# Attention in pairs of 64-row products, the low-rank mixer's sums after attention, the norm's preparation a step earlier

## The chip, the cores and the metric

The kernel runs on one core of a Trainium2 chip. The metric is device time in microseconds of one execution, the median of several runs. The engines are PE (TensorE, the matrix products, with its weight loads shown apart as PEld), DVE (VectorE), ACT (ScalarE), POOL (GpSimd) and SP (SyncE, which here only issues DMAs).

## The reference

Three blocks follow each other on a batch of 2, with 3136 tokens and 256 features, all in float32:

```
# 1 attention, z has 64 features
attn = max((z @ z.T) / S, 0) ** 2
x    = u * (attn @ v)
# 2 low-rank token mixer (rank 32), then a channel block of width 1024
u  = x + (x.T @ U @ V).T
x  = u + max(u @ w1a, 0) @ w2a
# 3 real part of a 2-d Fourier transform, norm, channel block of width 1024
u  = x + real(fft2(x));  un = (u - mean) / sqrt(var + 1e-6)
out = u + max(un @ w1b, 0) @ w2b
```

U, V and the channel weights are float64 and are converted on the chip. Every float32 factor is split into a high part h (rounded to the fast matmul format) and a low part l = x - h, and a product is the sum of h·h, h·l and l·h.

## The kernel before

The work is written out by hand in program order: each engine takes its instructions in the order in which Python emits them, and generators (`active`) are advanced once a step to weave side work in between.

**Attention** (`attention`) goes over 2 batches, 7 query chunks of 448 queries (`qc`), and 13 steps `p` of 256 keys (the last has 64 keys). `scores(b, qc, p)` fills a PSUM tile of two banks: T1 holds zh in rows 0 to 63 and zl in rows 64 to 127, T2 the same with the halves exchanged, so two products over all 128 rows (L541, L542) give all four parts for 128 keys. ACT then does Relu (L547) and Square (L550), DVE the high part (L551) and the low part (L96). `values(b, qc, p)` adds three products (L571, L573, L574) for each of two feature halves and two key tiles into two accumulators. In step 12 the 64 keys stand twice in the rows, so two score products and four value products do. Scores run two steps ahead of values (LAG = 2); at step 12, the turn, values come first, then `gate` (multiply by u, write to DRAM), then the scores. After the gate of a second chunk, `mixing` begins: PE transposes the gated tiles (L607), ACT and DVE split them, and PE sums them with U (L628), woven into attention's steps; the last ones (`tail`) run beside the first channel chunk. `finish_G` replicates the sums (L216). The conversions of the float64 weights are woven in as well; those of w1b (`conv_w`, not second) have a product with ones (L506).

**Channel blocks.** Fourteen chunks of 448 tokens for block 2 and fourteen for block 3, each in 8 steps: `hidden(k)` six products (L329 to L331), `project(k)` two steps later six more (L354 to L356). `Chunk.load` brings a chunk of x and of V from DRAM on SP; `prep1` or `prep2` runs during the chunk before, from its step 2, one piece a step: `prep1` adds the mixer's part, `prep2` makes the mean and the variance (row sum L302, three small DMAs on POOL's queue at L306, L319 and L321) and leaves 1/std in `rs`, which `finish` needs. `fourier(0)` and `fourier(1)` run beside the chunks; `features` waits for two `row` DMAs on POOL's queue (L953) that go out at the last of a group's pairs.

PSUM has eight banks: in attention two for misc and the mixer's sum (`pmg`), four for scores, two for the accumulators.

Of the kernel before, what the change touches and what calls it, by code (L numbers as in the profile page):

```python
# [15 lines left out]
ALU = mybir.AluOpType  # L16
# [66 lines left out]
def program(ctx, tc, zT, v, uT, U, V, w1a, w2a, w1b, w2b, b49, f64, fd, rep, mask, out):  # L83
# [18 lines left out]
    pmg = ctx.enter_context(tc.tile_pool(name="pmg", bufs=1, space=PSUM))  # L102
# [17 lines left out]
    V_d = dram.tile([RANK, S], F32, tag="Vd", name="Vd")  # L120
# [13 lines left out]
    Utail = const.tile([128, 4, 64], F32R, name="Utail")  # L134
# [67 lines left out]
    misc_pools = [(pmg, "m")]  # L202
# [8 lines left out]
    def finish_G(b, g, P):  # L211
        nc.vector.memset(P[64:128], 0.0)
        nc.vector.tensor_copy(P[0:64], g[0:64, 0:D])
        yield
        ps = pmg.tile([128, 512], F32, tag="m", name="ps_m")
# [7 lines left out]
    class Chunk:  # L223
# [4 lines left out]
        def load(self, a):  # L228
            self.a = a
            load(out=a, in_=aT_d[self.b][:, :, self.sl].rearrange("a p n -> p a n"))  # L230
            self.vr = com.tile([128, CH], F32, tag="Vr", name="Vr", bufs=1)
            for k in range(4):
                load(out=self.vr[k * 32 : k * 32 + 32, :], in_=V_d[:, self.sl])
# [4 lines left out]
        def prep1(self):  # L238
            b, a, vr = self.b, self.a, self.vr
            vs = com.tile([128, CH], F32R, tag="Vs", name="Vs", bufs=1)  # L240
            hcopy(vs, vr)
            for k in (32, 96):
                sub(vs[k : k + 32, :], vr[k : k + 32, :], f(vs[k : k + 32, :]))
# [30 lines left out]
        def prep2(self):  # L274
# [24 lines left out]
            yield  # L299

            ps = misc()
            mm(ps[0:1, 0:CH], ones[:, 0:1], st, start=True, stop=True)  # L302
            row = mp.tile([1, CH], F32, tag="vrow", name="vrow", bufs=1)
# [3 lines left out]
            yield  # L307
# [11 lines left out]
            late_dma(out=row_d.rearrange("(p j) -> p j", j=4), in_=y)  # L319
            self.rs = mp.tile([128, CH], F32, tag="rs", name="rs")  # L320
# [64 lines left out]
    def attention(stack):  # L385
# [5 lines left out]
        T1, T1d, T2, Vt, uq = {}, {}, {}, {}, {}  # L391
        zraw, vraw = {}, {}
        Uhl = att.tile([128, 25, 2, RANK], F32R, tag="U", name="Uhl", bufs=1)

        def load_z(b, c):
            raw = att.tile([128, CH], F32, tag="zraw", name="zraw")
            for h, dma in enumerate((load, nc.scalar.dma_start if (b, c) == (0, 0) else load)):
                dma(out=raw[h * 64 : h * 64 + 64, :], in_=zT[b, :, c * CH : c * CH + CH])
            zraw[b, c] = raw

        def split_z(b, c):
            raw = zraw.pop((b, c))
            if c == 0:
                T1[b] = big.tile([128, S], F32R, tag="T1", name=f"T1_{b}")
            dst = T1[b][:, c * CH : c * CH + CH]
            hcopy(dst, raw)
            if (b, c) == (0, 0):
                t = T2[0, 0] = att.tile([128, CH], F32R, tag="T2", name="T2")
                hcopy(t[64:128], raw[64:128])
                sub(dst[64:128], raw[64:128], f(dst[64:128]))  # L410
                sub(t[0:64], raw[0:64], f(dst[0:64]))
            else:
                sub(dst[64:128], raw[64:128], f(dst[64:128]))
            if c == NC - 1:
                T1d[b] = att.tile([128, 2, 64], F32R, tag="T1d", name=f"T1d_{b}")
                for h in range(2):
                    nc.vector.tensor_copy(T1d[b][:, h, :], f(T1[b][:, S - 64 : S]))

        def load_q(b, qc):
            t = att.tile([128, CH], F32R, tag="T2", name="T2")  # L420
            for h in range(2):
                nc.gpsimd.dma_start(
                    out=t[h * 64 : h * 64 + 64, :],
                    in_=T1[b][64 - h * 64 : 128 - h * 64, qc * CH : qc * CH + CH],
                )
            T2[b, qc] = t
# [24 lines left out]
        def conv_U(k):  # L451
# [14 lines left out]
            if k >= 3:  # L466
                o, i = ((3, 0), (0, 3))[k - 3]
                nc.vector.tensor_copy(
                    Utail[:, i : i + n - o], f(t[:, o:].rearrange("p a h n -> p a (h n)"))
                )  # L470

        def conv_V(k):
# [7 lines left out]
            load(out=quarter(V_d, 1), in_=y)  # L480

        def conv_w(src, k, second, dst):
# [13 lines left out]
            if not second:  # L496
                both = f(raw[:, 0:128])
                tt(out=both, in0=y[:, 0:128], in1=y[:, 128:256], op=ALU.add)
                yield
                yield  # L500
                while mixes:
                    yield
                mixes.append(k)

                ps = misc()
                mm(ps[:, 0:128], f(ones), both, start=True, stop=True)  # L506
                for a in range(2):
                    sub(y[:, a * 128 : a * 128 + 128], y[:, a * 128 : a * 128 + 128], ps[:, 0:128])
            load(out=dst[k], in_=y)
            if not second:  # L510
                yield
                mixes.remove(k)
# [17 lines left out]
        def scores(b, qc, p):  # L530
            n = 2 if p < 12 else 1
            ps = psS.tile([128, 2, 512], F32, tag="S", name="psS")
            q1 = T1[b][:, qc * CH : qc * CH + CH]
            q2 = T2[b, qc]
            for j in range(n):
                k = (
                    T1[b][:, (2 * p + j) * 128 : (2 * p + j) * 128 + 128]
                    if p < 12
                    else T1d[b].rearrange("p a n -> p (a n)")
                )  # L540
# [4 lines left out]
            parts = ((0, 1), (1, 1)) if (b, qc, p) == (0, 0, 0) else ((0, n),)  # L545
            for j, m in parts:
                act(out=c2(A)[:, j : j + m], in_=ps[:, j : j + m, 0:CH], func=AF.Relu, scale=1.0 / S)  # L547
            for j, m in parts:
                w = slice(j * CH, (j + m) * CH)
                act(out=A[:, w], in_=A[:, w], func=AF.Square)  # L550
                nc.vector.tensor_copy(h[:, w], A[:, w])  # L551
                if p < 12:
                    sub(l[:, w], A[:, w], f(h[:, w]))
                else:
                    sub(h[64:128, w], A[64:128, w], f(h[64:128, w]))
            prob[b, qc, p] = (h, l)

        acc = {}

        def values(b, qc, p):  # L560
            if p == 0:
                acc[b, qc] = [psO.tile([128, 512], F32, tag=f"O{a}", name=f"psO{a}") for a in range(2)]
            o = acc[b, qc]
            h, l = prob.pop((b, qc, p))
            vt = Vt[b, p]
            for a in range(2):
                dst = o[a][:, 0:CH]
                for j in range(2 if p < 12 else 1):
# [489 lines left out]
```

## Time and profile before

| | |
|---|---|
| median of 3 runs | 1218.4 us (1217.89 to 1220.7) |
| the profiled execution | 1218.11 us |
| its span in the trace | 1216.3 us |
| PE busy, PEld busy | 99%, 91% of the span |
| DVE, ACT, POOL busy | 68%, 54%, 4% |
| DMA | 68.56 MB, mean 56 GB/s |

The span is the time between the first and the last instruction of the trace; the device time has 1.8 us around it. PE's busy time is a union of overlapping products, so the spacing of their starts tells more than their lengths. Attention takes the first half, the channel blocks the second.

### The profile page before, as it was taken

To read this page: it belongs to the slowest core of one execution; us is meant where nothing else is said; L and a number is where in the kernel's file an instruction comes from. 1 tells how busy PE (TensorE), PEld (TensorE's weight loads), DVE (VectorE), ACT (ScalarE), POOL (GpSimd) and SP (SyncE) were. 2 spreads that over 40 slices of the span, in tenths; PEclk is the share of its full clock that TensorE was granted. 3 is DMA by queue.
4 is the path that set the end of the run, shared out by engine and by line. 5 is a ranking of instruction groups with operands and counts; after the bars stand their busy time and mean duration, and the time that the engine had idled before them with its cause. 6 is when DMAs were issued, how large, how long until landed. Compare 5 with 4: busy or idle time off the path is not lost.

```text
span 1216.3 us, 16363 instructions
## 1 busy us (share of the span) xinstructions
PE 1202.9 (99%) x6038; PEld 1102.4 (91%) x6038; DVE 829.8 (68%) x1565; ACT 652.5 (54%) x1052; POOL 46.8 (4%) x94
## 2 busy tenths in 40 slices
PE   9999999999999999999999999999999999999998
PEld 7999999999999999999899998999989889999997
DVE  7867777888666667666555456476576688666664
ACT  7767667777666566665433334333255444444442
POOL 0000000000000000000000000000000101000100
PEclk9999999999999999999999999999999999999999
DMA  5302220333122012211111102212012111111111
GB/s 153 104 22 69 68 64 26 117 93 105 44 64 64 9 57 77 60 40 54 38 51 53 46 23 85 81 45 62 5 57 73 48 39 31 39 31 38 31 39 46
DMA packets 58688, 68.56 MB, mean 56 GB/s; under 512 B 11630, under 2 KB 53712, under 8 KB 58608
## 3 DMA queue, kind: packets, MB, share of 16 engines
q1 hardware_dynamic: 54144, 61.13, 16.4%
q0 software_dynamic: 4384, 6.27, 2.6%
q8 instruction: 47, 0.77, 0.3%
q14 instruction: 33, 0.27, 0.1%
q10 hardware_dynamic: 80, 0.11, 0.0%
HBM read 44.86 MB, written 19.56 MB: 53 GB/s over the span
## 4 chain that ended last, share of the span: by engine, by line
PE 90%; DVE 4%; issue 3%; DMA 1%; ACT 1%; POOL 0%; SPq 0%; DVEq 0%; POOLq 0%; ACTq 0%
PE psO L574 12%; PE psO L571 12%; PE psO L573 11%; PE psH L330 6%; PE psH L329 6%; PE psH L331 6%; PE psC L355 6%; PE psC L354 6%; PE psC L356 6%; PE psS L542 6%; PE psS L541 6%; PE ps_g L628 1%; PE ps_m L607 1%; DVE Hl L335 1%; DVE l L96 0%
## 5 line engine op out<-in xcount | busy, mean ns | idle before, releaser
L571 PE MATMUL psO<-h,Vt 128*128 128x448 f32 x700 | 256.6, 367 | 0.1
L574 PE MATMUL psO<-h,Vt 128*128 128x448 f32 x700 | 256.5, 366 | 0.0
L573 PE MATMUL psO<-l,Vt 128*128 128x448 f32 x672 | 246.3, 367 | 0.3 <-DVE l L96 0.2
L547 ACT ACTIVATE P<-psS 128x896 f32<-128x896 f32 (+1 forms) x183 | 161.6, 884 | 147.7 <-PE psS L542 147.2
L335 DVE SCALAR_TENSOR_TENSOR Hl<-psH,Hh 128x448 fp32r<-128x448 f32 x224 | 139.6, 623 | 142.7 <-ACT Hh L334 141.6
L334 ACT ACTIVATE Hh<-psH 128x448 fp32r<-128x448 f32 x224 | 121.8, 544 | 200.2 <-PE psH L331 197.1
L96 DVE TENSOR_TENSOR l<-P,h 128x896 fp32r<-128x896 f32 (+1 forms) x197 | 201.2, 1021 | 23.5 <-ACT h L93 17.7
L551 DVE CAST h<-P 128x896 fp32r<-128x896 f32 (+1 forms) x183 | 111.0, 606 | 145.7 <-ACT P L550 144.6
L550 ACT ACTIVATE P<-P 128x896 f32<-128x896 f32 (+1 forms) x183 | 168.4, 921 | 5.7
L329 PE MATMUL psH<-h,w 128*128 128x448 f32 x448 | 167.9, 375 | 0.0
L330 PE MATMUL psH<-l,w 128*128 128x448 f32 x448 | 164.5, 367 | 0.2 <-DVE l L96 0.2
L331 PE MATMUL psH<-h,w 128*128 128x448 f32 x448 | 164.5, 367 | 0.0
L355 PE MATMUL psC<-Hl,w 128*128 128x448 f32 x448 | 163.7, 365 | 0.0
L354 PE MATMUL psC<-Hh,w 128*128 128x448 f32 x448 | 163.7, 365 | 0.0
L356 PE MATMUL psC<-Hh,w 128*128 128x448 f32 x448 | 163.2, 364 | 0.0
L571 PEld LDWEIGHTS psO<-h,Vt 128*128 128x128 f32 x700 | 131.6, 188 | 11.4 <-DVE aT L586 0.6
L574 PEld LDWEIGHTS psO<-h,Vt 128*128 128x128 f32 x700 | 131.6, 188 | 11.2 <-DVE Vt L96 0.3
L573 PEld LDWEIGHTS psO<-l,Vt 128*128 128x128 f32 x672 | 126.4, 188 | 11.3 <-DVE l L96 0.9
L541 PE MATMUL psS<-T 128*128 128x448 f32 x336 | 125.2, 373 | 0.8 <-DVE T L96 0.8
L542 PE MATMUL psS<-T,T 128*128 128x448 f32 x336 | 124.2, 370 | 0.0
L329 PEld LDWEIGHTS psH<-h,w 128*128 128x128 f32 x448 | 84.7, 189 | 7.9 <-ACT h L93 0.3
L331 PEld LDWEIGHTS psH<-h,w 128*128 128x128 f32 x448 | 84.4, 188 | 7.3
(276 smaller groups left out, 1421.8 us busy)
## 6 DMA issues: line engine op xcount, KB each, us to landing
uT<-in_uT SPq DMA_DIRECT2D x14, 448.0 KB, 4.2
vraw<-in_v SPq DMA_DIRECT2D x24, 256.0 KB, 2.7
out<-P SPq DMA_DIRECT2D x27, 224.0 KB, 2.0
aTd<-aT SPq DMA_DIRECT2D x13, 448.0 KB, 3.0
P<-aTd SPq DMA_DIRECT2D x13, 448.0 KB, 3.6
scr<-wst SPq DMA_DIRECT2D x16, 256.0 KB, 2.0
Vr<-Vd SPq DMA_DIRECT2D x56, 56.0 KB, 3.0
rs<-rsd POOLq DMA_DIRECT2D x14, 224.0 KB, 3.6
```

Source lines behind the costliest of these rows:

```text
L96: tt(out=o, in0=a, in1=b, op=ALU.subtract)
L329: mm(ps[:, 0:CH], wh, self.h[:, a], start=a == 0, stop=False)
L330: mm(ps[:, 0:CH], wh, self.l[:, a], start=False, stop=False)
L331: mm(ps[:, 0:CH], wl, self.h[:, a], start=False, stop=a == 1)
L354: mm(dst, wh, h, start=k == 0, stop=False)
L355: mm(dst, wh, l, start=False, stop=False)
L356: mm(dst, wl, h, start=False, stop=k == 7)
L541: mm(ps[:, j, 0:CH], k, q1, start=True, stop=False)
L542: mm(ps[:, j, 0:CH], k, q2, start=False, stop=True)
L571: mm(dst, vh, hj, start=p == 0 and j == 0, stop=False)
L573: mm(dst, vh, lj, start=False, stop=False)
L574: mm(dst, vl, hj, start=False, stop=p == 12)
```

## The change

Attention's products take 64 rows each. Keys 0 to 127 of a step lie in rows 0 to 63 of KT and keys 128 to 255 in rows 64 to 127, and the queries stand in both halves, so the scores are three products (h·h, l·h, h·l) for each half, issued alternately. The value products are cut into their upper and lower 64 rows, each with an accumulator of its own; `gate` adds the two. At step 12 the scores have 224 columns, and feature half 1 of step 11 is put behind feature half 0 of step 12. The queries are read from DRAM again for every chunk and split (at steps 4 and 8) instead of copied on POOL's queue.

```diff
 def scores(b, qc, p):
-    for j in range(n):
-        mm(ps[:, j, 0:CH], k, q1, start=True, stop=False)
-        mm(ps[:, j, 0:CH], k, q2, start=False, stop=True)
+    w = CH if p < 12 else CH // 2
+    for kk, kq in ((0, 0), (1, 0), (0, 1)):
+        for j, r in enumerate(halves):
+            ...
+            mm(ps[:, j, 0:w], k, q[r, kq, o : o + w], start=(kk, kq) == (0, 0), stop=kq == 1)
+def products(b, qc, p, a):
+    if p < 12:
+        todo = [(j, (a, k, x), (a, k, x)) for j in range(2) for k, x in ((0, h), (0, l), (1, h))]
+    elif a == 0:
+        todo = [(0, (0, 0, h), (0, 0, l)), (0, (0, 1, h), (1, 1, h))]
+    else:
+        todo = [(0, (1, 0, h), (1, 0, l))]
+    for n, (j, *both) in enumerate(todo):
+        for i, (fa, k, x) in enumerate(both):
+            r = halves[i]
+            mm(o[fa][i][:, 0:CH], vt[r, j, k, fa * 128 : fa * 128 + 128], x[r, j * CH : j * CH + CH], ...)
 def gate(b, qc):
+    t = att.tile([128, 2, CH], F32, tag="aT", name="aT")
     for a in range(2):
-        tt(out=t[:, a], in0=o[a][:, 0:CH], in1=u[:, a], op=ALU.mult)
+        hcopy(t[:, a], o[a][0][:, 0:CH])
+        tt(out=t[:, a], in0=o[a][1][:, 0:CH], in1=t[:, a], op=ALU.add)
+    tt(out=t, in0=t, in1=u, op=ALU.mult)
     load(out=aT_d[b][:, :, qc * CH : qc * CH + CH].rearrange("a p n -> p a n"), in_=t)
```

The mixer no longer runs beside attention, nor does w1b's product with ones (it moves into `weights(0)`, beside channel chunks 2 to 5). All of x is read into SBUF in four DMAs behind attention, after four short early ones for the first 1536 tokens of batch 0; the mixer of both batches then runs before the first channel chunk, and the chunks take x from there. The four early DMAs go out at step 11 of the last query chunk; `first` is what is left of batch 0's mixer and then the first chunk's `prep1`.

```diff
+                    if p == NP - 2:
+                        for k in range(4):
+                            t = ptile().rearrange("p (a n) -> p a n", a=2)[:, :, 0:384]
+                            load(out=t, in_=aT_d[0][:, :, k * 384 : k * 384 + 384].rearrange("a p n -> p a n"))
+                            early.append(t)
+    for b in range(NB):
+        for s in (slice(1536, S), slice(0, 1536)):
+            load(out=xT[b][:, :, s], in_=aT_d[b][:, :, s].rearrange("a p n -> p a n"))
+    def mixer(b):
+        for k in range(25):
+            ps = misc()
+            for a in range(2):
+                ...
+                nc.tensor.transpose(ps[:, a * 128 : a * 128 + 128], t, ident)
+            hcopy(h, ps[:, 0:D])
+            sub(l, ps[:, 0:D], f(h))
+            ready.append((k, h, l))
+            if k > 1:
+                sums(*ready.pop(0))
+        ...
+        yield from finish_G(b, g, ...)
+        mix0, mix1 = mixer(0), mixer(1)
+        for _ in range(13):
+            next(mix0)
+        last_G = mix0
+        opening = [mix1, first()]
+        while opening:
+            for g in list(opening):
+                if next(g, "end") == "end":
+                    opening.remove(g)
```

V is split once when it is converted and is loaded as h and l on POOL's queue. In `prep2` one step is put between the stacked squares and the row sum L302, one is taken away behind the DMA of the variances, and one is put between the write of 1/std to DRAM and the DMA that reads it back into `rs`; it begins at step 1 of the chunk before and not at step 2. In `fourier` the first transposes come a step later, and the `row` DMAs go out at a group's first pair (in the first group at its second):

```diff
-                if g == pairs[-1]:
+                if g == max(1, pairs[0]):
...
-            if k == 2 and c + 1 < len(chunks):
+            if c + 1 < len(chunks) and k == 3 - chunks[c + 1].layer:
...
                 active.insert(0, chunks[c + 1].prep())
```

The products that warm PE up at the start become twenty 64-row ones.

## Rows read from the trace of the kernel before

**Rows 1.** The page: span, busy engines, bytes per slice, chain of waits
```profile
span 1216.3 us, 16363 instructions
PE 1202.9 (99%) x6038; PEld 1102.4 (91%) x6038; DVE 829.8 (68%) x1565; ACT 652.5 (54%) x1052; POOL 46.8 (4%) x94
...
GB/s 153 104 22 69 68 64 26 117 93 105 44 64 64 9 57 77 60 40 54 38 51 53 46 23 85 81 45 62 5 57 73 48 39 31 39 31 38 31 39 46
...
PE 90%; DVE 4%; issue 3%; DMA 1%; ACT 1%; POOL 0%; SPq 0%; DVEq 0%; POOLq 0%; ACTq 0%
```

**Rows 2.** Groups by line, PE: count, busy us, mean ns, idle before
```profile
L506 PE MATMUL ps_m<-stg,ones 128*128 128x128 f32 x16 | 3.1, 273 | 0.0
```

**Rows 3.** Timeline, PE, twelve value products: start us, length us
```profile
591.17 0.36 PE L571 MATMUL psO<-h,Vt 128*128 128x448 f32 x1
...
593.61 0.36 PE L250 MATMUL ps_m<-Vs,Gs 128*128 128x448 f32 x1
```

**Rows 4.** Timeline, PE, two products that follow each other
```profile
767.18 0.37 PE L354 MATMUL psC<-Hh,w 128*128 128x448 f32 x1
767.39 0.37 PE L355 MATMUL psC<-Hl,w 128*128 128x448 f32 x1
```

**Rows 5.** Timeline, PEld (weight loads), the same stretch and 0.8 us on
```profile
767.18 0.19 PEld L355 LDWEIGHTS psC<-Hl,w 128*128 128x128 f32 x1
...
767.80 0.19 PEld L822 LDWEIGHTS ps_x<-nl,b49h 98*128 98x128 f32 x1
767.91 0.19 PEld L823 LDWEIGHTS ps_x<-nh,b49l 98*128 98x128 f32 x1
768.02 0.19 PEld L329 LDWEIGHTS psH<-h,w 128*128 128x128 f32 x1
```

**Rows 6.** Timeline, PE, four transposes and four sums of the mixer
```profile
104.34 0.60 PE L607 MATMUL ps_m<-ident,aT 128*128 128x128 f32 x4
...
105.25 0.37 PE L541 MATMUL psS<-T 128*128 128x448 f32 x1
```

**Rows 7.** Groups by line, ACT and DVE, splits of 256 columns
```profile
L93 ACT CAST anh<-ps_m 128x256 fp32r<-128x256 f32 x8 | 3.0, 373 | 5.5 <-PE ps_m L607 5.5
...
L96 DVE TENSOR_TENSOR Tl<-ps_x,Th 128x256 fp32r<-128x256 f32 x10 | 4.2, 417 | 0.0
```

**Rows 8.** Windows: busy us of each engine, then PEclk, DMA share, GB/s
```profile
555.00:560.00 5.00, 5.00 (x26) 4.54 (x25) 3.58 (x6) 4.25 (x5) 0.00 (x0) 1.00 0.64 203
950.00:960.00 10.00, 7.44 (x31) 6.76 (x30) 4.47 (x10) 3.90 (x8) 1.60 (x3) 0.83 0.13 27
```

**Rows 9.** DMA issues by line: count, KB each, median us from issue to landing
```profile
P<-aTd SPq DMA_DIRECT2D x13, 448.0 KB, 3.6
```

**Rows 10.** Timeline, DVE, around a turn
```profile
174.12 1.09 DVE L96 TENSOR_TENSOR l<-P,h 128x896 fp32r<-128x896 f32 x1
175.13 1.15 DVE L586 TENSOR_TENSOR aT<-psO,uT 128x448 f32<-128x448 f32 x2
177.59 0.63 DVE L551 CAST h<-P 128x896 fp32r<-128x896 f32 x1 [1.31 <-ACT P L550]
```

**Rows 11.** Timeline, ACT, around the same turn
```profile
175.65 0.92 ACT L547 ACTIVATE P<-psS 128x896 f32<-128x896 f32 x1 [2.23 <-PE psS L542]
176.60 0.95 ACT L550 ACTIVATE P<-P 128x896 f32<-128x896 f32 x1
```

**Rows 12.** Timeline, PE, waits behind attention (in brackets)
```profile
955.48 0.66 PE L894 MATMUL ps_x<-row,fN 128*128 128x384 f32 x1 [2.56 <-DMA row<-ecl]
...
988.88 0.36 PE L302 MATMUL ps_m<-sm,ones 128*1 128x448 f32 x1 [1.52 <-DVE sm L96]
```

**Rows 13.** Timeline, POOL's queue, before the second of these waits
```profile
951.36 0.58 POOL L321 DMA_DIRECT2D rs<-rsd  x1 [1.40 <-DMA rsd<-vy]
...
952.45 0.51 POOL L953 DMA_DIRECT2D row<-ecl  x1
```

**Rows 14.** Timeline, DVE, the last chunk's end
```profile
1210.36 0.63 DVE L371 TENSOR_TENSOR P<-psC,rs 128x448 f32<-128x448 f32 x1 [1.97 <-DMA rs<-rsd]
```

More of the change, by code (lines that the diff above doesn't have):

```diff
@@ L226, in __init__, with load @@
             self.sl = slice(c * CH, c * CH + CH)
[L228 to L233, printed above, removed]
+        def load(self):
+            self.vs = com.tile([128, CH], F32R, tag="Vs", name="Vs", bufs=1)
+            for k in (0, 64):
+                late_dma(out=self.vs[k : k + 64, :], in_=V_d[:, self.sl])
         def prep(self):
@@ L238, in prep1 @@
         def prep1(self):
[L239 to L243, printed above, removed]
+            b, vs = self.b, self.vs
+            a = late["xT"][b][:, :, self.sl]
             yield
@@ L299, in prep2 @@
             yield
+            yield
             ps = misc()
             mm(ps[0:1, 0:CH], ones[:, 0:1], st, start=True, stop=True)
-            row = mp.tile([1, CH], F32, tag="vrow", name="vrow", bufs=1)
+            row = late["small"]()[0:1]
             hcopy(row, ps[0:1, 0:CH])
@@ L401, in split_z @@
[L401 to L417, printed above, removed]
@@ L419, in load_q, with load_z @@
-        def load_q(b, qc):
[L420 to L426, printed above, removed]
+        KT, KTl, Q, Vt, uq = {}, {}, {}, {}, {}
+        zraw, qraw, vraw = {}, {}, {}
+        halves = (slice(0, 64), slice(64, 128))
+        def load_z(b, i):
+            raw = att.tile([128, 3, 128], F32, tag="zraw", name="zraw")
+            for j, r in enumerate(halves):
+                if i < 4:
+                    src = zT[b, :, i * 768 : i * 768 + 768].rearrange("d (p j n) -> d j p n", j=2, n=128)
+                    load(out=raw[r], in_=src[:, j])
+                else:
+                    load(out=raw[r, 0, 0:64], in_=zT[b, :, S - 64 : S])
+            zraw[b, i] = raw
@@ L479, in conv_V @@
             y = yield from words(raw, 128, 196)
-            load(out=quarter(V_d, 1), in_=y)
+            h, l = (raw[:, i * 196 : i * 196 + 196].bitcast(F32R) for i in range(2))
+            hcopy(h, y)
+            sub(l, y, f(h))
+            for i, x in enumerate((h, l)):
+                late_dma(out=quarter(V_d[i * RANK : i * RANK + RANK], 1), in_=x)
         def conv_w(src, k, second, dst):
@@ L548, in scores @@
             for j, m in parts:
[L549 to L555, printed above, removed]
+                x = slice(j * w, (j + m) * w)
+                act(out=A[:, x], in_=A[:, x], func=AF.Square)
+                nc.vector.tensor_copy(h[:, x], A[:, x])
@@ L576, in attention @@
[L576 to L583 removed]
+                acc[b, qc] = [
+                    [psO.tile([128, 512], F32, tag=f"O{a}{i}", name=f"psO{a}{i}") for i in range(2)] for a in range(2)
+                ]
@@ L715, in attention @@
                 if turn:
-                    last = (b, qc) == (1, NC - 1)
-                    gate(b, qc, last)
+                    gate(b, qc)
                     ahead(i + LAG)
-                    if not last and (qc % 2 or qc == NC - 1):
-                        active.append(mixing(b, qc))
                 if b == 0 and qc == NC - 1:
@@ L740, in attention @@
         assert not active and next(jobs, None) is None
-        def tail():
-            for tiles in groups(NC - 1):
-                x = mix(1, NC - 1, tiles, True)
-                yield
-                yield
-                mix2(1, NC - 1, tiles, *x, True)
-                yield
-            yield from finish_G(1, gacc[1], late["mp"].tile([128, 512], F32, tag="wst", name="wst")[:, 0:D])
-        return tail
+        return early
     def pair_late():
@@ L851, in fourier @@
                 tokens(i - 1)
+            if i == 0:
+                yield
             if i == 7:
@@ L971, in weights @@
         ts = {}
-        for k in range(10):
+        for k in range(12):
             if k < 8:
@@ L975, in weights @@
                 load(out=ts[k], in_=wb_d[i][k])
-            if k >= 2:
+            if i == 0 and 1 < k < 10:
+                y = ts[k - 2].rearrange("p (a n) -> p a n", a=2)
+                both = mp.tile([128, 128], F32, tag="both", name="both", bufs=1)
+                tt(out=both, in0=y[:, 0], in1=y[:, 1], op=ALU.add)
+                yield
+                ps = misc()
+                mm(ps[:, 0:128], f(ones), both, start=True, stop=True)
+                for a in range(2):
+                    sub(y[:, a], y[:, a], ps[:, 0:128])
+                wb[i].split(k - 2, ts.pop(k - 2))
+            elif 1 < k < 10:
                 wb[i].split(k - 2, ts.pop(k - 2))
```

282 lines of the change are left out of this document (126 added, 156 removed).

## The prediction

> **What bounds the kernel now.** I read the page first: PE is busy for 99% of the 1216.3 us span, and the chain of waits runs through PE for 90% of it [rows 1]. No other engine is above 68%. So the time is the number of PE products times their spacing, plus the few places where PE waits, and an edit is worth what it takes out of PE's queue, less what makes PE wait. The length of one product (0.37 us) is not its price, since products overlap. The price is the distance of starts: twelve value products begin within 593.61 - 591.17 = 2.44 us, 0.203 us each [rows 3]. Then the weight loads: beside products of 448 columns they keep the same rhythm, but behind products of only 32 columns loads follow each other at 767.80, 767.91 and 768.02, so a load of 128 columns has a floor of 0.111 us, with 98 rows as with 128 [rows 5]. Last the waits of PE behind attention [rows 12] and the chunk that ends the kernel [rows 14].
>
> **Attention.** A full step has 4 score and 12 value products, 16 slots of 0.203 us. After the change it has 3 + 12 pairs of half products. If the two halves of a pair run side by side, a pair takes one slot, and each of the 2 x 7 x 12 = 168 full steps saves 0.203 us: 34.1 us. The last step has 2 + 4 slots now; it gets three value pairs and three score pairs of 224 columns, which I put at the load floor, 0.111 us: 6 x 0.203 - 3 x 0.203 - 3 x 0.111 = 0.28 us, and 14 of them save 3.9 us. Together **-38.0 us**.
>
> All of it hangs on the price of a pair, and the trace has no 64-row product. The bounds: a slot can't be under 448 columns at 2.4 GHz, the level of the granted clock here, 0.187 us, which over 168 x 15 + 14 x 3 = 2562 pairs would be 41 us better still. From above: a pair needs two loads. If loads go one after the other also for different halves, a pair takes 2 x 0.111 = 0.222 us [rows 5]. If a half's load can't lie under its own product, it takes 0.203 + 0.111 = 0.314 us; if halves run in turn, 0.406 us. I take 0.203 us: it is the row nearest to it, each partition still streams 448 columns and 128 weights per slot as now, and the load of the next product demonstrably runs under the product of the same rows (the load for L355 begins at 767.18 with the product L354, and L355 follows 0.21 us later [rows 4, 5]).
>
> The Trainium skill, "TensorE: Matmul & The Clock Gate", section on the mechanism of row and column tiling, says that a weight load overlaps with products in flight only when the row group differs. By that rule the change would cost 0.314 us a pair. The rows just named speak against it: there the load has the row group of the product that is running, all 128 rows, and the spacing stays at 0.21 and not 0.31. The skill's "TensorEngine Tiling (Array Packing)", under its key properties, says that different tiles can do weight loads and products in parallel; no row here shows it.
>
> **The turn.** The accumulators are single, so the next chunk's first value products wait for `gate`. Count from the start of step 11 on PE: scores 0.61, feature half 0 of step 11 1.22, half 0 of step 12 0.41 (2.24), half 1 of both 1.42 (3.66), scores of two steps 1.22: at 4.9 us PE wants the first accumulator pair. Meanwhile the scores of 0.61 go through Relu 0.92, Square 0.95, cast 0.63 and difference 1.09 [rows 10, 11], some 0.2 us of handing over, and DVE is free at about 4.5; the new addition (0.6, as L586's 0.57 each [rows 10]) ends at 5.2. So PE waits 0.3 us at 13 turns: **+4 us**, with bounds of 0 and, if the additions come one DVE instruction later, 1.0 us each, 13 us. ACT's copies are hidden by its own idle time (2.23 us before that Relu [rows 11]); DVE's extra work per chunk, some 3 us, is covered by its share of 68%.
>
> **Mixer and w1b's product out of attention.** Four transposes and four sums take 105.25 - 104.34 = 0.91 us of PE [rows 6], 0.455 us a tile of 128 tokens. 46 tiles are woven into attention, 20.9 us, and 4 beside the first channel chunk, 1.8 us; with the products of `finish_G` and of the first `prep1`, about 1.2 us by width, **-23.9 us**. The 16 products of L506 [rows 2] leave and come back in `weights(0)`: nothing.
>
> **The opening** takes their place with nothing beside it. Count from attention's last product. The last gate (copy 0.55, addition 0.6, multiplication 1.1 over 896 columns) and SP's issue put the four big loads at 2.9 us, because they stand behind the gate's own store on SP's queue. A 448 KB load lands 3.6 us after its issue [rows 9]. The best stretch moved 203 GB/s at a busy share of 0.64 [rows 8], 317 GB/s at full share; at that rate 448 KB take 1.5 us, so 2.1 us are latency, and 2 x 128 x 2 x 3136 x 4 bytes = 6.42 MB take 20.3 us, with the store's 1.4 us between. All are in at 26.7 us. Batch 0's mixer runs before (12 tiles from the early loads, 13 when the first big load is in, done by about 18). Batch 1's begins with its first tokens, and these come with the last load: it starts at 26.7. A tile costs 0.455 us of PE, 0.37 of ACT and 0.42 of DVE [rows 6, 7]; with handing over I take 0.5 us, 12.5 us for 25. `finish_G`, on which the first channel product does not depend but behind which it is queued, adds 1.2 us. PE has then waited some 8 us; a wait of 2.56 us was followed by a stretch with a granted clock of 0.83 [rows 8, 12], 1.7 us lost in 10, and I add 2 us. In sum **+42 us**, bounds: 27 us if the loads never hold it (25 us of mixing and the end), and 64 us at 153 GB/s, the highest slice of the page [rows 1], where the 6.42 MB take 42 us.
>
> **Waits that go.** The wait for the `row` DMA: POOL's queue stood 1.40 us for `rsd` before it could issue L953 [rows 13]; issued up to three steps sooner, the rows are there. 2.56 us plus the 1.7 us at the lower clock: -4.2 us [rows 8, 12]. L302's wait for DVE, 1.52 us, gets a step more: -1.5. At the end `rs` comes from POOL's queue without standing for `rsd`, so the last L371 need not wait for it at 1210.36 [rows 14]; its accumulator is done some 0.7 us sooner: -0.7. **-6.4 us**. What is late next there is the chain of DVE halves and the output DMA, as now. Loading V on POOL's queue (28 DMAs, two a chunk, a chunk ahead) puts them before `vv` and `rsd` only in the two chunks that follow the last loads, so I cost it at nothing; where it is not hidden, it is 0.5 us of issue each.
>
> **Sum.** -38.0 - 23.9 + 42 + 4 - 6.4 = -22.3 us: a span of 1194.0, and with the 1.8 us around the span (1218.11 against 1216.3) 1195.8. The profiled execution stands 0.3 us below the median of 1218.4, so I say **1196 us**.
>
> **Rivals.**
>
> *Loads in turn.* If the loads of the two halves share one path, a pair takes 0.222 us: 2562 x 0.019 = 48.7, and the 42 short pairs 0.111 more each, 4.7. That ends at 1196 + 53 = 1249, slower than before. For it: the floor of 0.111 us does not shrink for 98 rows [rows 5], so it may be paid per load whatever its height; PEld is already busy 91% [rows 1]. Against it: nothing in the trace shows two loads of different rows competing. It decides from a pair price of 0.203 + 22.3 / 2562 = 0.212 us: above that the change loses.
>
> *The opening is longer.* At 153 GB/s it takes 22 us more, 1218. If PE stays at the lower clock through batch 1's mixer, its products cost 0.91 us a tile, PE-bound, 10 us more, 1206; both, 1228. For it: the long waits before it, the clock's fall after 2.56 us. Against it: at 955 the clock came back under dense products, and the mixer is dense on PE.
>
> *A half's load not under its own product* (the skill's rule above): 0.111 us more for each pair, 2562 x 0.111 = 284 and 4 for the short ones, 1484. The rows with all 128 rows contradict it.
>
> *The halves run in turn* and the change does not do what it says: 0.203 more a pair, 520 + 5 us, 1721.
>
> **How the numbers follow.** The likeliest case, pairs at about one slot and an opening near 42 us, has 0.66; its own range is 1172 to 1215, from the pair (4 ns either way is 10 us), the opening (27 to 50) and the turn (0 to 13). A longer opening has 0.10, loads in turn 0.18, the two others 0.03 each. To leave out no more than 2 in 10, the range must reach to the loads in turn: 1172 to 1252. A change of 0.3% (3.7 us) is about what a measurement here can tell from none: faster means under 1214.7, slower over 1222.1. Of the first case nearly all is faster (0.65), of the longer opening 0.07, with 0.02 the same: 0.72 faster, 0.03 the same, 0.25 slower.
>
> **What would show it.** The first score products of a steady step: six starts within 0.61 us, two of them together each time, says that halves run side by side; starts of weight loads of different halves a few ns apart say that loads do too, 0.11 us apart that they go in turn. Attention should be some 57 us shorter (38.0 + 20.9 + 1.8 - 4), and a gap of about 0.3 us before the first value product of a chunk is the turn. In the opening, PE should stand twice for the big loads, the second time longer, and the first channel product should come about 42 us after attention's last. At L894 no DMA wait. The prediction is wrong if a pair takes over 0.212 us, or if the opening is over 64 us.

## The result and the profile after

The changed kernel takes 1207.2 us, the median of four runs (1205.7 to 1207.9), against 1218.1 us before (1217.5 to 1220.7): a ratio of 0.9908, with an interval of 0.9896 to 0.992. It is faster by 10.9 us, half of the 22.3 forecast. The profiled execution took 1207.9 us, its span is 10.2 us shorter than before [rows 1].

The page of the kernel after, its answer to [rows 1], and one of its groups of PE (line, operation, count, busy us, mean ns, idle before):

```profile
span 1206.1 us, 21307 instructions
PE 1180.0 (98%) x8488; PEld 1080.5 (90%) x8488; DVE 831.5 (69%) x1581; ACT 662.6 (55%) x1102; POOL 52.7 (4%) x104
...
GB/s 133 103 17 88 89 65 71 58 139 118 81 51 92 44 40 39 1 45 282 8 16 17 29 9 61 60 26 33 8 49 81 49 45 28 39 31 39 32 39 46
...
PE 82%; DVE 9%; ACT 4%; DMA 3%; issue 2%; SPq 0%; DVEq 0%; ACTq 0%
...
L567 PE MATMUL psO<-h,Vt 64*128 64x448 f32 x2744 | 434.7, 366 | 2.2 <-DVE aT L594 1.5
```

The chain of waits now has 82% on PE and 9% on DVE, where it had 90% and 4%: work left PE's queue, and part of the room went to waits. The slice at 282 GB/s is the opening; no slice before was above 153. Split at the last value product and at the first product of the channel blocks, the span compares like this:

| piece | before | after | measured | forecast |
|---|---|---|---|---|
| to the last value product | 597.0 | 549.1 | -47.9 | -54.9 (-38.0 + 4 - 20.9) |
| the opening | 0.2 | 43.2 | +43.0 | +42 |
| from the first channel product | 619.1 | 613.8 | -5.3 | -9.4 (-1.8 - 1.2 - 6.4) |
| span | 1216.3 | 1206.1 | -10.2 | -22.3 |

**Attention.** The timeline of PE in a steady stretch of the kernel after (start, length), to be held against [rows 3], and behind it PEld, the weight loads, of the same stretch:

```profile
129.66 0.36 PE L567 MATMUL psO<-l,Vt 64*128 64x448 f32 x1
129.66 0.77 PE L567 MATMUL psO<-h,Vt 64*128 64x448 f32 x4
130.07 0.57 PE L567 MATMUL psO<-l,Vt 64*128 64x448 f32 x2
130.27 0.57 PE L567 MATMUL psO<-h,Vt 64*128 64x448 f32 x2
130.48 0.77 PE L535 MATMUL psS<-Q,KT 64*128 64x448 f32 x5
```

```profile
129.86 0.18 PEld L567 LDWEIGHTS psO<-h,Vt 64*128 64x128 f32 x1
129.86 0.39 PEld L567 LDWEIGHTS psO<-l,Vt 64*128 64x128 f32 x2
```

Two products start at 129.66, and two loads at 129.86: the halves run side by side, and so do their loads. The groups follow at 130.07, 130.27 and 130.48, in steps of one or two times 0.205 us. Over all pairs without a wait the mean is 0.2047 us (0.2036 for a product before); the short pairs of 224 columns take some 0.11.

The turn, DVE's two additions in the kernel after, beside [rows 10]:

```profile
127.44 1.15 DVE L594 TENSOR_TENSOR aT<-psO,aT 128x448 f32<-128x448 f32 x2
```

The first addition ends near 128.0. At such a turn PE's pairs are late by some 0.27 us in all.

**The opening.** PE's waits there in the kernel after (in brackets), ACT's, SP's first two issues, the big loads' median us from issue to landing, and the windows of the stretch (busy us of PE, PEld, DVE, ACT and POOL, granted clock, DMA share, GB/s):

```profile
558.38 0.47 PE L733 MATMUL psC<-nh,Uhl 128*64 128x256 f32 x1 [6.73 <-ACT nh L93]
...
575.91 0.67 PE L215 MATMUL ps_x<-wst,repc 128*128 128x256 f32 x2 [0.57 <-DVE wst L212]
...
580.41 0.44 PE L744 MATMUL ps_g<-ident,xT 128*128 128x128 f32 x2 [1.12 <-DVE nl L96]
```

```profile
557.95 0.37 ACT L93 CAST nh<-ps_m 128x256 fp32r<-128x256 f32 x1 [7.91 <-DMA aTd<-aT]
```

```profile
549.53 0.36 SPq L724 DMA_DIRECT2D xT<-aTd  x1
551.85 0.36 SPq L596 DMA_DIRECT2D aTd<-aT  x1
```

```profile
xT<-aTd SPq DMA_DIRECT2D x2, 1600.0 KB, 8.4
xT<-aTd SPq DMA_DIRECT2D x2, 1536.0 KB, 10.4
```

```profile
552.10:558.40 6.30, 0.02 (x1) 0.02 (x1) 0.04 (x1) 0.45 (x2) 0.41 (x3) 0.50 1.02 396
558.40:562.30 3.90, 3.90 (x17) 3.62 (x18) 2.30 (x6) 1.59 (x5) 0.73 (x2) 0.50 1.01 417
...
582.80:586.20 3.40, 3.34 (x16) 3.34 (x17) 1.80 (x6) 1.12 (x3) 0.00 (x0) 0.50 0.00 0
```

The long wait is not for a load of x. ACT's first cast of the mixer writes `nh`, whose place in SBUF was the last gate's `aT`; it waits 7.91 us until the store of that tile (L596) has landed, which shares the DMA engines with a load of 1.6 MB (L724) issued 2.3 us ahead of it. PE stands with it, its granted clock goes to the lower level (0.50, 1.2 GHz) and stays there 3.9 us into the mixer. Batch 1's mixer (571.5 to 591.9) never waits for its tokens, but with the pieces of `finish_G` and `prep1` woven in it takes 20.4 us, 3.4 of them at the lower clock (582.80 to 586.20). That second fall is this execution's: e6 and e8 below, with the same opening, have none, and their openings take 42.2 us. The window of e8 from the clock's rise to the first channel product:

```profile
563.00:591.20 28.20, 24.92 (x179) 19.76 (x178) 21.45 (x52) 16.61 (x46) 1.03 (x2) 0.99 0.26 98
```

**Behind it.** PE's new wait in the channel blocks of the kernel after, and what DVE does ahead of it:

```profile
980.58 0.44 PE L349 MATMUL psC<-Hh,w 128*128 128x448 f32 x1 [1.42 <-DVE P L372]
```

```profile
976.91 1.93 DVE L909 TENSOR_TENSOR xT<-xT,A 128x12 f32<-128x12 f32 x6
978.74 1.16 DVE L330 SCALAR_TENSOR_TENSOR Hl<-psH,Hh 128x448 fp32r<-128x448 f32 x2
979.80 1.16 DVE L372 TENSOR_TENSOR P<-psC,rs 128x448 f32<-128x448 f32 x2
```

Both waits of [rows 12] are gone. Instead PE waits for the accumulator that L372 still reads, and L372 stands behind the six additions of the Fourier step on DVE. At the end of the kernel DVE's wait for `rs` [rows 14] is gone too; the same instruction now waits for PE's last products alone:

```profile
1200.61 0.62 DVE L366 TENSOR_TENSOR P<-psC,rs 128x448 f32<-128x448 f32 x1 [1.20 <-PE psC L351]
```

### The profile page after: what moved, and what is told of

Same layout as the page of the kernel before. It is cut to its first block, busy times and chain, and to the rows that moved or that the text cites. A ratio compares the mean times of both kernels' runs of the same rounds, so it can differ in the third digit from the quotient of the medians.

```text
span 1206.1 us, 21307 instructions
## 1 busy us (share of the span) xinstructions
PE 1180.0 (98%) x8488; PEld 1080.5 (90%) x8488; DVE 831.5 (69%) x1581; ACT 662.6 (55%) x1102; POOL 52.7 (4%) x104
## 3 DMA queue, kind: packets, MB, share of 16 engines
q1 hardware_dynamic: 52896, 60.72, 15.9%
## 4 chain that ended last, share of the span: by engine, by line
PE 82%; DVE 9%; ACT 4%; DMA 3%; issue 2%; SPq 0%; DVEq 0%; ACTq 0%
PE psO L567 29%; PE psH L324 7%; PE psH L326 7%; PE psH L325 7%; PE psC L350 7%; PE psC L349 7%; PE psC L351 7%; PE psS L535 7%; PE psC L733 1%; DMA vraw<-in_v 1%; ACT P L544 1%; DVE Hl L330 1%; ACT P L541 1%; DVE h L545 1%; DVE Vt L96 1%
## 5 line engine op out<-in xcount | busy, mean ns | idle before, releaser
L567 PE MATMUL psO<-h,Vt 64*128 64x448 f32 x2744 | 434.7, 366 | 2.2 <-DVE aT L594 1.5
L567 PEld LDWEIGHTS psO<-h,Vt 64*128 64x128 f32 x2744 | 279.2, 185 | 24.6 <-DVE aT L594 4.9
L567 PE MATMUL psO<-l,Vt 64*128 64x448 f32 x1372 | 274.5, 368 | 1.3 <-DVE l L96 1.3
L96 DVE TENSOR_TENSOR l<-P,h 128x896 fp32r<-128x896 f32 (+2 forms) x211 | 209.9, 995 | 24.0 <-ACT h L93 17.7
L349 PE MATMUL psC<-Hh,w 128*128 128x448 f32 x448 | 163.7, 365 | 1.4 <-DVE P L372 1.4
L350 PE MATMUL psC<-Hl,w 128*128 128x448 f32 x448 | 163.7, 365 | 0.9 <-DVE Hl L330 0.9
L567 PEld LDWEIGHTS psO<-l,Vt 64*128 64x128 f32 x1372 | 143.0, 185 | 13.8 <-DVE l L96 3.8
L535 PE MATMUL psS<-Q,KT 64*128 64x448 f32 x1002 | 130.5, 363 | 2.2 <-ACT KT L93 1.9
L535 PEld LDWEIGHTS psS<-Q,KT 64*128 64x128 f32 x1002 | 99.0, 185 | 8.7 <-ACT KT L93 2.4
L349 PEld LDWEIGHTS psC<-Hh,w 128*128 128x128 f32 x448 | 84.0, 188 | 9.5 <-issue 1.9
L350 PEld LDWEIGHTS psC<-Hl,w 128*128 128x128 f32 x448 | 84.1, 188 | 9.1 <-DVE Hl L330 2.1
```

The lines of the kernel that those rows point to most:

```text
L96: tt(out=o, in0=a, in1=b, op=ALU.subtract)
L349: mm(dst, wh, h, start=k == 0, stop=False)
L350: mm(dst, wh, l, start=False, stop=False)
L535: mm(ps[:, j, 0:w], k, q[r, kq, o : o + w], start=(kk, kq) == (0, 0), stop=kq == 1)
L567: mm(o[fa][i][:, 0:CH], vt[r, j, k, fa * 128 : fa * 128 + 128], x[r, j * CH : j * CH + CH], start=p == 0 and n == 0, stop=p == 12 and (a = ...
```

## The experiments

**e1: value products of 128 rows again.** Scores stay in halves, values go back to whole products with one accumulator each:

```diff
-    todo = [(j, (a, k, x), (a, k, x)) for j in range(2) for k, x in ((0, h), (0, l), (1, h))]
+    todo = [(j, k, x) for j in range(2) for k, x in ((0, h), (0, l), (1, h))]
...
-    r = halves[i]
-    mm(o[fa][i][:, 0:CH], vt[r, ...], x[r, ...])
+    mm(o[a][0][:, 0:CH], vt[:, ...], x[:, ...])
```

> The changed kernel with its value products on all 128 rows again and two accumulators (gate as before); the scores stay in halves. The output is still the reference's. Theory A, the change of rows between scores and values costs PE something each time: two changes a step, each at least the part of a product that can't overlap (0.366 - 0.203 = 0.16 us), 182 x 2 x 0.16 = 58 us, so about 1265 us. Theory B, the change of rows is free and only the scores had to be cut: the value slots cost 0.203 us as before, four instead of three in the last steps (14 x 0.2 = 2.9 us more), a shorter gate (some 2 us less): 1207 to 1209 us.

1263.6 us, ratio 1.0382 (1.0365 to 1.040); attention, from the first score product to the last value product, takes 601.1 us, not 544.7. PE's timeline in e1:

```profile
131.62 0.37 PE L565 MATMUL psO<-l,Vt 128*128 128x448 f32 x1
131.82 0.37 PE L565 MATMUL psO<-h,Vt 128*128 128x448 f32 x1
132.12 0.88 PE L535 MATMUL psS<-Q,KT 64*128 64x448 f32 x6
132.93 0.47 PE L565 MATMUL psO<-h,Vt 128*128 128x448 f32 x1
133.24 0.36 PE L565 MATMUL psO<-l,Vt 128*128 128x448 f32 x1
```

Among themselves the products keep 0.20 us. From 128 rows to 64 the step is 0.30, and the three pairs from 132.12 to 132.93 take 0.81 instead of 0.61; behind the way back it is 0.31. Two changes a step, some 0.2 us each, over 168 steps are 67 us by this sum; 56 are measured, 0.17 each. Halving the scores alone would have lost, since it saves 34 us by the prediction's sum and the changes of rows cost 56: the value products, which gain nothing by themselves, had to follow.

**e10: the halves one after the other.** In each group all products of the upper rows are issued, then all of the lower rows:

```diff
+    order = [(n, i) for n in range(len(todo)) for i in range(2)]
+    if p < 12:
+        order.sort(key=lambda x: x[1])
```

> The changed kernel, but the six value products of a step and feature half are issued first for rows 0 to 63 and then for rows 64 to 127, not alternately. Theory A, halves run side by side only where they follow each other in PE's queue: each of the 168 full steps has 24 value products of 0.203 us in turn and not 12 pairs, less an overlap of one product at each change, so 2.0 to 2.4 us more a step, 340 to 410 us, 1550 to 1620 us in all. Theory B, PE takes products of the free half ahead: 1207 us.

1214.1 us (one run), attention 6.6 us longer than in the changed kernel and not doubled. PE's timeline in e10:

```profile
130.63 0.37 PE L535 MATMUL psS<-Q,KT 64*128 64x448 f32 x1
130.72 0.36 PE L571 MATMUL psO<-h,Vt 64*128 64x448 f32 x1
130.83 0.36 PE L535 MATMUL psS<-Q,KT 64*128 64x448 f32 x1
130.93 0.36 PE L571 MATMUL psO<-l,Vt 64*128 64x448 f32 x1
131.04 0.36 PE L535 MATMUL psS<-Q,KT 64*128 64x448 f32 x1
```

One half is in the score products of a step while the other still works on value products that stand ahead of them in program order: each half has its own sequence, at its own 0.205 us. Alternating them in the program is worth a few us, not a factor of two for the value products.

**e2: the last gate's tile elsewhere.** Only its place in SBUF changes, to one that the opening does not use:

```diff
+    if (b, qc) == (1, NC - 1):
+        t = f(c2(ctile("h", F32R)))
+    else:
         t = att.tile([128, 2, CH], F32, tag="aT", name="aT")
```

> The changed kernel with the last gate's result in a tile of a pool that lives to the end, so that nothing behind attention lies over it. In the changed kernel ACT waits 7.9 us, from the last gate to the landing of the gate's store, before it may write the mixer's first tile. Theory A, that wait goes, batch 0's mixer begins at about 551 and not 558, but batch 1's mixer then waits for its first tokens, which land with the last of the four big loads, at about 569 (20 us behind attention) against 571.3 now: 1205 us. Theory B, the wait stands on the path in full: 1200 us.

1205.5 us, ratio 0.9902 (0.9887 to 0.9916), the opening 40.5 us instead of 43.2 (42.2 in e6 and e8). The mixer begins at 553.2, but then PE's timeline in e2 shows

```profile
571.11 0.44 PE L747 MATMUL ps_x<-ident,xT 128*128 128x128 f32 x2 [3.95 <-DMA xT<-aTd]
```

and that is the wait that the prediction had counted on: batch 1's first tokens come with the last load, 21.5 us after attention (549.6). The store's wait had covered it.

**e3: those tokens loaded second.** On top of e2:

```diff
-    for b in range(NB):
-        for s in (slice(1536, S), slice(0, 1536)):
-            load(out=xT[b][:, :, s], ...)
+    lo, hi = slice(0, 1536), slice(1536, S)
+    for b, s in ((0, hi), (1, lo), (0, lo), (1, hi)):
+        load(out=xT[b][:, :, s], ...)
```

> The gate tile moved, and the four big loads in the order in which the mixers take them (batch 0 from token 1536, batch 1 to 1536, batch 0 to 1536, batch 1 from 1536). Theory A, the loads' order holds batch 1's mixer: with it both mixers run through, the opening is 7 us shorter than in the changed kernel, 1200 us, and PE stays at the higher clock in it. Theory B, ACT's and DVE's order in the woven part sets the end: 1204 to 1205 us.

1201.4 us, ratio 0.9856 (0.9834 to 0.9879). The opening takes 36.0 us. The windows of e3 (columns as above):

```profile
553.00:568.90 15.90, 14.93 (x115) 12.15 (x114) 12.55 (x32) 10.52 (x30) 0.26 (x1) 1.00 1.01 403
568.90:575.60 6.70, 5.04 (x31) 3.69 (x31) 4.80 (x12) 3.49 (x10) 1.02 (x2) 1.00 0.24 65
575.60:579.00 3.40, 3.15 (x16) 3.15 (x16) 1.81 (x6) 1.15 (x4) 0.00 (x0) 0.50 0.00 0
```

At 553.0 to 568.9 PE is busy 94% under full DMA load. The two faults, the second hidden by the first, made 6 to 7 us together: 43.2, or the 42.2 of e6 and e8, less 36.0. The loads' order alone was not run; in the changed kernel PE has no wait for tokens that it could have removed. What is left is the stretch with the woven pieces and the 3.4 us at the lower clock behind it.

**e5: the woven pieces behind the mixers.**

```diff
-        opening = [mix1, first()]
-        while opening: ...
+        for opening in (mix1, first()):
+            for _ in opening:
+                pass
```

> The changed kernel; in the opening batch 1's mixer runs to its end before the rest of batch 0's mixer and the first chunk's preparation, which were woven into it. In the changed kernel batch 1's mixer took 20.4 us (571.5 to 591.9) where 25 tiles of 0.455 us of PE make 11.4. Theory A, the woven pieces hold it up through ACT's and DVE's order and three PSUM tiles: alone it takes 12.5 to 14 us, and finish_G and the two pieces of prep1 behind it about 5 us: 1203 to 1205 us. Theory B, the tiles' own chain (transposes, ACT, DVE, sums) or the lower clock sets 0.8 us a tile: it takes 18 to 20 us alone and the pieces come on top: 1210 to 1213 us.

1210.4 us, ratio 0.9942 (0.9927 to 0.9956). Batch 1's mixer alone takes 12.2 us (571.7 to 583.9, at full clock), the prediction's 12.5. But PE's timeline in e5 behind it is

```profile
587.19 0.67 PE L215 MATMUL ps_m<-wst,repc 128*128 128x256 f32 x2 [1.72 <-DVE wst L212]
588.78 0.74 PE L244 MATMUL ps_x<-Vs,Gs 128*128 128x448 f32 x1 [0.92 <-DVE Gs L96]
...
590.84 0.74 PE L324 MATMUL psH<-h,w 128*128 128x448 f32 x1 [0.94 <-ACT h L93]
```

with the first channel products at the lower clock. `finish_G` and `prep1` are a chain over DVE, ACT and PE of some 7 us (583.9 to 590.8). Woven in, it comes to about the same: 20.4 us, less 12.2 for the mixer alone and 1.7 for the lower clock, leave 6.5.

**e12: the pieces at every second pair of tiles.** On top of e3:

```diff
-while opening:
+for n in range(99):
     for g in list(opening):
-        if next(g, "end") == "end":
-            opening.remove(g)
+        if g is mix1 or mix1 not in opening or n % 2:
+            if next(g, "end") == "end":
+                opening.remove(g)
```

> The same base (gate's last tile elsewhere, low tokens of batch 1 second), and in the opening one piece of batch 0's finish and of the first chunk's sum stands behind every second pair of batch 1's tiles, not behind each. Theory A: the four waits of PE between 570 and 576 us (0.3, 1.3, 0.6, 0.6) and the granted clock's fall to the lower level at 575.6 to 579 come from these pieces, crowded on DVE and ACT behind the first tiles: the opening is 32 to 33.5 us instead of 36.0, in all about 1198. Theory B: each piece costs its wait wherever it stands: the opening stays within 1 us of 36, in all 1201.

1198.9 us (1197.9 to 1202.3), ratio 0.9844 (0.983 to 0.9857). The interval overlaps that of e3, whose runs spread as far (1197.3 to 1201.9), so the time can't decide between the theories. In the trace (an execution of 1202.3 us) the opening takes 36.2 us. The waits stand in pairs elsewhere:

```profile
579.18 0.33 PE L736 MATMUL psC<-nh,Uhl 128*64 128x256 f32 x1 [0.43 <-ACT nh L93]
579.90 0.33 PE L736 MATMUL psC<-nl,Uhl 128*64 128x256 f32 x1 [0.39 <-DVE nl L96]
```

The granted clock falls not among the pieces but at the start of the opening (554.4). That is not the edit's doing, for e11 below, with the pieces as in e3, has its fall at the start too and none later (columns as above):

```profile
548.20:551.60 3.40, 3.34 (x15) 3.06 (x16) 1.94 (x5) 1.54 (x6) 0.54 (x2) 0.51 0.99 363
551.60:580.50 28.90, 25.63 (x186) 20.35 (x185) 22.30 (x54) 17.23 (x48) 1.02 (x2) 1.00 0.51 200
```

So there are four traces with one fall of the clock each, two with the pieces behind every pair (e3 36.0 us, e11 35.9) and two behind every second (e12 36.2, e13 36.0). They speak for Theory B: each piece brings its wait along. Why a piece on ACT and DVE costs PE more than its own work there stays open.

**e4: batch 1's mixer beside the channel chunks.** With e2's tile; the mixer of batch 1 starts at step 3 of the first chunk, with a PSUM bank of its own.

```diff
-        opening = [mix1, first()]
-        while opening: ...
+        for _ in first():
+            pass
+        starts[3] = mix1
```

> The gate tile moved, and batch 1's mixer taken out of the opening and woven beside the first channel chunks, two tiles a step from step 3 (its sums in a bank of their own, the other misc tiles two until it ends). Theory A, the opening is then batch 0's mixer, finish_G and prep1, about 19 us (549 to 568), and batch 1's mixer costs only its PE time, 25 x 0.455 = 11.4 us: 592.3 - 568 - 11.4 = 13 us less, 1194 us. Theory B, beside the chunks the tiles wait for ACT, DVE and two PSUM tiles and hold PE's queue: 1200 us or more.

1202.7 us, ratio 0.9872 (0.9858 to 0.9887). The opening falls to 20.1 us, as expected, but what follows grows by 17.0 us, not 11.4. The window of e4 at the start of the chunks:

```profile
569.50:575.70 6.20, 6.18 (x14) 4.43 (x15) 2.38 (x4) 1.48 (x3) 0.20 (x1) 0.50 0.21 53
```

PE is busy there for all of 6.2 us, at the lower clock: half of it, 3.1 us, is lost. The other 2.5 us of the difference I didn't follow to rows. Putting the mixer beside other work is no better than running it through.

**e6: the norm as before.** `prep2` begins at step 2 again, with its steps as they were, and the `row` DMAs go out at a group's last pair.

```diff
-                if g == max(1, pairs[0]):
+                if g == pairs[-1]:
...
-            if c + 1 < len(chunks) and k == 3 - chunks[c + 1].layer:
+            if c + 1 < len(chunks) and k == 2:
```

> The changed kernel with the small edits of the channel blocks undone: prep2 begins at step 2 with its steps as before, the row DMAs go out at a group's last pair, the first transposes of the Fourier part come a step sooner. Theory A, these edits bring the 6.4 us that the prediction gave them: 1213 us, with a wait for the row DMA and a stretch of lower clock near the second Fourier group. Theory B, the waits that went came back elsewhere (the changed kernel has 1.6 us at a chunk's accumulators and 0.9 us at a project product that the kernel before has not): 1207 to 1209 us.

1209.2 us, ratio 0.9933 (0.9918 to 0.9948): 2 us above the changed kernel, with intervals that touch. In the traces the part behind the opening is 3.7 us longer (617.5 against 613.8; in nine traces of kernels that leave this part alone it lies between 613.8 and 614.0). That the medians differ by less goes with attention and the opening, which vary by 1 to 2 us between executions. The waits of [rows 12] are back on PE in e6, whose L871 and L296 are the L894 and L302 of before, and L349 no longer waits; at the kernel's end DVE waits for `rs` again, 2.01 us at L365, the L371 of before. PE's two waits:

```profile
947.43 0.42 PE L871 MATMUL ps_g<-row,fN 128*128 128x384 f32 x1 [2.94 <-DMA row<-ecl]
...
980.53 0.37 PE L296 MATMUL ps_x<-sm,ones 128*1 128x448 f32 x1 [1.55 <-DVE sm L96]
```

**e8: conversions every third step, not every second.** Some 5 us in attention's chunks 1, 2, 5, 6 and 7 were still without a cause.

```diff
-                if i >= 9 and i - started[-1] >= 2 and ...
+                if i >= 9 and i - started[-1] >= 3 and ...
```

> The changed kernel with a conversion of the float64 weights begun every third attention step at most, not every second. In the changed kernel a regular query chunk takes 38.15 us, but the chunks 0, 1, 2, 5, 6 and 7 together 7 us more, with waits of values for DVE. Theory A, the conversions' pieces stand ahead of the squares and differences on ACT and DVE: 2 to 4 us less, 1203 to 1205 us. Theory B, the splits of v, z and q and their DMAs are what stands there: 1206 to 1208 us.

1206.5 us, ratio 0.9903 (0.9887 to 0.9919), attention 544.7 us as in the changed kernel. Counted from one gate to the next, chunk 1 loses its extra 0.5 us, but chunks 5 and 6 take 39.7 and 40.7 us, where they take 39.6 and 40.6 in the changed kernel: for most of the 5 us it isn't the conversions.

**e11: splits two steps behind their loads.** On top of e3, three raw buffers for z and v, and

```diff
-    if p > 0:
-        split_z(1, p - 1)
+    if p > 1:
+        split_z(1, p - 2)
...
-    if p > 0:
-        split_v(1, p - 1)
+    if p > 1:
+        split_v(1, p - 2)
```

> The kernel with the gate's last tile elsewhere and batch 1's low tokens loaded second, and in attention the splits of the second batch's z and v come two steps behind their loads instead of one (three raw buffers). Open is where some 5 us in chunks 1, 2, 5, 6 and 7 of attention come from. Theory A: a step became shorter (16 slots to 15), the lead of one step is 3.07 us now, a load of this size lands later than that, so ACT stands before its split and the scores behind it are late: with two steps chunk 5, 6 and 7 lose their extra 1.4, 0.8 and 1.9 us, attention ends 3 to 4 us sooner (about 545.5 instead of 549), in all about 1198. Theory B: it is the splits' own work on ACT and DVE, whenever it comes: attention ends within 1 us of 549, in all 1201.

1196.4 us, ratio 0.982 (0.9807 to 0.9834). Attention ends at 544.7 us from the start of the span instead of 549.2; in seven traces with attention as in the changed kernel it ends between 547.5 and 550.4. ACT's waits from 160 to 320 us (in us, times, longest), first in the changed kernel, with the landing time of the z loads, then in e11:

```profile
ACT Vt L93 <- DMA vraw<-in_v: 5.3, 4, 2.6
...
ACT KT L93 <- DMA zraw<-in_zT: 2.7, 2, 2.1
...
zraw<-in_zT SPq DMA_DIRECT2D x16, 96.0 KB, 3.7
```

```profile
ACT KT L93 <- DMA zraw<-in_zT: 0.2, 1, 0.2
```

A load of z lands 3.7 us after its issue, and a step is 15 pairs of 0.2047, 3.07 us: a split one step behind its load stands on ACT's queue, and the Relu of the next scores behind it. For v this account is not complete: its loads land after 2.8 us in the median, less than a step, and yet ACT waits for four of them; with the longer lead these waits are gone. Chunks 5 and 6 lose their extra 1.5 and 0.8 us, chunks 0 and 1 together 2.1. In those two only the number of buffers differs, not the lead, so that the third buffer lets loads go out sooner; a third buffer without the longer lead was not run. Chunk 7 keeps its 1.7 us: at its first turn a split of v stands ahead of the gate's additions on DVE, and PE waits 1.2 us for them.

**e13: e11 and e12 together, and the keys split ahead of the values at the start.**

```diff
-        split_v(0, 0)
         split_z(0, 0)
+        split_v(0, 0)
```

> Both of these together, and at the very start the keys split ahead of the values (ACT waits 2.5 us there for the values' first tile and PE 1.85 us for the keys). If the costs are what they seem and add up: 3 to 4 us from the splits, 2.5 to 4 from the opening, 0.6 to 1 at the start, in all 1193 to 1196. If the pieces only move their waits: 1200 to 1202.

1194.9 us, ratio 0.9802 (0.9789 to 0.9815), the fastest of all, 12 us below the changed kernel. It can't be told from e11 by the intervals; the opening is 36.0 us as in e3, and attention ends 0.5 us sooner than in e11. The time lies in the range of costs that add up, but the 2.5 to 4 us from the opening did not come.

## Why the prediction was right, and where its steps failed

1196 us was forecast, in a range of 1172 to 1252, and 1207.2 came. The mechanism, a pair of half products in the slot of one whole product, is what happened. The sum of the span was 12.1 us too good: 7.0 in attention, 1.0 in the opening and 4.1 behind it.

**The pair: right.** One slot a pair was forecast, 0.203 us, and 0.2047 measured. The 1.1 ns more than a product before cost 2562 x 0.0011 = 2.8 us. Loads in turn (0.222) and a load not under its own product (0.314) are out by the rows at 129.66 and 129.86. The Trainium skill, "TensorE: Matmul & The Clock Gate", in the section on the mechanism of row and column tiling, also says that products keep strict program order. e10's rows contradict it for products of different rows: starts there are out of program order, and the time is 1214 us, where halves in strict order were expected at 1550 or more.

**The turn: right.** 0.3 us was forecast, 0.27 came at a regular turn. At chunk 7's first turn the additions come one DVE instruction later, as the prediction's upper bound had it (1.0 us): PE waits 1.2 us there.

**Attention's term: too large.** -47.9 came where -54.9 was forecast. (The "some 57 us shorter" among the signs counts in the 1.8 us of the tail, which ran beside the first channel chunk.) The gap is larger still, because w1b's products with ones leave this piece for the next. The prediction put their going and coming together at nothing, which is right for the whole but not for the pieces; in the trace of the kernel before, two of these products move the next one by 0.14 us, and 16 of them are 1.1 us:

```profile
297.53 0.38 PE L506 MATMUL ps_m<-stg,ones 128*128 128x128 f32 x2
297.67 0.45 PE L541 MATMUL psS<-T 128*128 128x448 f32 x1
```

Of these 8.1 us, 2.8 are the pair's price. The step that failed is that the prediction counted ACT's and DVE's busy shares ("DVE's extra work per chunk, some 3 us, is covered by its share of 68%") and gave the lead of the loads no term. The step shrank from 16 slots to 15, the splits' lead of one step with it, and a split that waits for its DMA holds ACT's queue. e11, with the longer lead and the third buffers, takes 4.5 us of attention back, and chunk 7's first turn holds 1.7 more. With the pair's price these make 9.0, which fits 8.1 as far as traces agree (attention's end varies by 3 us between executions).

**The opening: the sum right by luck.** +42 was forecast and +43.0 came, but from other terms. Batch 1's mixer began 22.4 us after attention's last product and not 26.7, and from there to the first channel product it took 20.8 us and not 15.7: two errors of 4 and 5 us that cancel. Loads were put at 317 GB/s and 26.7 us; they moved 396 to 417 and were in after 21.5 (e2). They do not all stand behind the gate's store on SP's queue, as the prediction had it: the first goes out 2.3 us ahead of it. "PE should stand twice for the big loads" failed: it stood once, 6.7 us, for the landing of that store, which the prediction had seen only as one item on SP's queue; and batch 1's mixer, at 0.49 us a tile alone (e5), took 20.4 us and not 12.5 + 1.2, because the chain of `finish_G` and `prep1` was priced by its width on PE, 1.2 us, where it is some 7 us of hand-overs. At the lower clock the mixer ran 3.9 us at half speed, which costs about 2 as forecast, and in the profiled execution 3.4 us more later, which cost 1.7.

**Waits that go: mis-sized.** -6.4 was forecast, e6 shows about 3.7 in the trace. The waits for the row DMA, at L302 and at the kernel's end went as told. What the prediction left out is what is late next in the middle of the stretch: PE has new waits of 1.4 us at L349 and 0.9 at L350, both for DVE. Behind the opening -9.4 was forecast and -5.3 came: 2.7 of these 4.1 us are this term (6.4 - 3.7), and 1.1 are w1b's products, which come back here.

## What to carry to other kernels

Price a chain that crosses engines by its hand-overs and not by its width on the busiest engine, and when a step becomes shorter, recount in us every lead that is written in steps. Follow each buffer that is reused when a stage ends back to the DMA that last reads it: its store may wait behind the next stage's loads. If a product with half the rows is to run beside another, give all products of the stretch the same rows.

## What the hardware showed that was not expected

- The two halves of PE's rows run as two sequences: products of one half start ahead of earlier ones of the other, and e10, which issues 2016 pairs of value products half by half, lost only 6.6 us (one run).
- A change between products of 128 and of 64 rows costs 0.17 to 0.2 us each way (e1: 56 us over 336 changes; in the rows, steps of 0.30 and 0.31 us where 0.20 is usual, and 0.81 for three pairs). The Trainium skill, "TensorEngine Tiling (Array Packing)", key properties, says that a change of tiling mode drains the engine; e1's rows agree and give the price.
- Four loads of 1.5 to 1.6 MB kept 396 to 417 GB/s for 10 us in the changed kernel and 403 for 15.9 us in e3, where the best window of before had 203 at a busy share of 0.64 [rows 8]. The gate's own store of 448 KB, 2.9 us to landing in the median of all 14, took 6 among them (issued at 551.85, waited for until 557.95).
